# Block-sparse attention and a squared-ReLU feed-forward on one core: transposed scores, the mask in the contraction, row sums from a ones column, and two layers interleaved

## The chip, the core and the metric

The kernel runs on one core of one Trainium2 chip. The metric is the device time of one execution in microseconds (us). A profile of one execution gives, for each engine, every instruction's start, duration and what released it. PE is the matrix engine (TensorE), PEld its weight load, DVE is VectorE, ACT is ScalarE, POOL is GpSimd, SP is the engine whose queue issues most transfers here. The span of the profiled execution is 1.4 to 2.3 us shorter than its run time; stage lengths below are parts of the span.

## The reference

There are 4 batches, 8 heads, 768 tokens and 64 values per head. A query block of 32 tokens sees its neighbour blocks, the first and the last block, and three random blocks. The first and the last query block see everything. The result is reshaped to 3072 x 512 and goes through a two-layer feed-forward part with 2048 hidden units.

```python
scores = scale * np.matmul(q, k.transpose(0, 1, 3, 2))       # scale = 1/8
mask = np.abs(blk_i - blk_j) <= window                        # window = 1, blocks of 32
mask = mask | (blk_i == 0) | (blk_j == 0) | (blk_i == n_blocks - 1) | (blk_j == n_blocks - 1)
for qb in range(n_blocks):
    for kb in sampled_blocks[qb]:                             # 3 random blocks
        mask[qb * block:(qb + 1) * block, kb * block:(kb + 1) * block] = True
scores = np.where(mask, scores, -1000000000.0)
attn = softmax(scores)                                        # shortened
x = (attn @ v).transpose(0, 2, 1, 3).reshape(B * S, H * D)
h = x @ w_in
r = np.maximum(h, 0.0)
return (r * r) @ w_out
```

## The kernel before

It has three parts, one after the other. First a mask of 128 x 6 x 768 numbers is built. Then attention treats one tile of 128 queries and one head at a time: there are 192 such tiles. Queries lie on the partitions, so the probabilities have to be transposed before they can be multiplied with the values. Last comes the feed-forward part, for which the weights are loaded and cast in one go.

```python
# one tile of attention; 4 batches x 4 head pairs x 6 query tiles x 2 heads
ps_sc = psAsc.tile([P, S], F32, name="ps_sc", tag="ps_sc")          # one buffer
nc.tensor.matmul(ps_sc[:, :512], lhsQ, kT[hl][:, :512], start=True, stop=True)
nc.tensor.matmul(ps_sc[:, 512:], lhsQ, kT[hl][:, 512:], start=True, stop=True)
nc.scalar.activation(out=sc, in_=ps_sc, func=AF.Exp, scale=scale)
# ... cut
nc.vector.tensor_tensor_reduce(out=scb, in0=sc, in1=mask_add[:, qi, :], scale=1.0, scalar=0.0,
                               op0=AOP.mult, op1=AOP.add, accum_out=row_sum)
nc.vector.reciprocal(out=inv_sum, in_=row_sum)
for tch in range(TCH):                                              # 6 times
    nc.tensor.transpose(ps_tr, scb[:, tch * P:(tch + 1) * P], identb)
    nc.vector.tensor_copy(out=aT, in_=ps_tr)
    nc.tensor.matmul(ps_o, aT, vT[hl][:, tch, :], start=(tch == 0), stop=(tch == TCH - 1))
nc.vector.tensor_scalar_mul(out=pair_out[:, hl * D:(hl + 1) * D], in0=ps_o, scalar1=inv_sum)
# ... cut: output transpose and its copy into xT_sb

# feed-forward, after all of attention; 6 x 16 times
# ... cut: four matmuls into ps_gT
nc.scalar.activation(out=g, in_=ps_gT, func=AF.Relu)
nc.scalar.activation(out=gb, in_=g, func=AF.Square)
for ts in range(tw_per):
    nc.tensor.matmul(ps_y[ts], gb[:, ts * P:(ts + 1) * P], w_out_sb[:, nch, :],
                     start=(nch == 0), stop=(nch == NF - 1))
```

The softmax here doesn't subtract the row's maximum and nothing guards it: scores larger than these inputs give would overflow.

## Time and profile before

The median of three runs is 892.4 us; the span of the profiled one is 891.0 us.

| stage | span, us | what fills it |
|---|---|---|
| set-up | 0 to 63 | mask on DVE and PE |
| attention | 63 to 703 | 192 tiles at 3.33 us; PE and DVE both about 80% busy |
| feed-forward | 703 to 891 | PE 94% busy, DVE almost idle |

Over the span PE is busy for 730.3 us, DVE for 553.8, ACT for 270.2 and POOL for 4.5. Such a table must not be read as "PE has 18% to spare": in attention a tile is handed from PE to ACT to DVE to PE, and each waits for the other. The prediction below shows the lines for this.

### The profile page before, as it was taken

Reading aid. Unit: us, or ns where it says so; the run is one execution under the profiler, and the core shown is the slowest. Engines: PE = TensorE matmul, PEld = TensorE weight load, DVE = VectorE, ACT = ScalarE, POOL = GpSimd, SP = SyncE. Lnnn points to the kernel's source line nnn. Section 1 sums busy time; section 2 is a strip of 40 time slices with the busy share of each in tenths; the row PEclk is TensorE's granted clock in tenths of the full one; section 3 lists DMA queues with packets and bytes.
Section 4 is the critical chain, followed back from the end, with each engine's and each line's share of the span. In section 5 each row is a group of like instructions: output and inputs, shape, how many; then the busy total and the mean of one; then the engine's idle time right before and its main releaser. Section 6 shows DMA issues by size and latency. Waiting matters only on the chain.

```text
span 891.0 us, 12152 instructions
## 1 busy us (share of the span) xinstructions
PE 730.3 (82%) x3969; PEld 351.4 (39%) x3985; DVE 553.8 (62%) x2609; ACT 270.2 (30%) x385; POOL 4.5 (1%) x21
## 2 busy tenths in 40 slices
PE   3878878787888778787888778787878899999996
PEld 1223444444343444444343444444443333333332
DVE  6547877878787877878787878878786400110111
ACT  0013122131312222131313222121313266666664
POOL 2000000000000000000000000000000000000000
PEclk9999999999999999999999999999999999999999
DMA  9800101021120202021120202020100001110111
GB/s 273 263 0 1 28 1 36 1 54 30 25 54 1 54 1 54 1 54 27 28 47 8 54 0 54 1 54 22 24 1 0 1 1 48 47 48 1 48 47 48
DMA packets 81411, 34.33 MB, mean 39 GB/s; under 512 B 75716, under 2 KB 75716, under 8 KB 80836
## 3 DMA queue, kind: packets, MB, share of 16 engines
q1 hardware_dynamic: 81348, 33.56, 14.3%
q8 instruction: 31, 0.51, 0.2%
q14 instruction: 32, 0.26, 0.1%
HBM read 27.26 MB, written 6.29 MB: 38 GB/s over the span
## 4 chain that ended last, share of the span: by engine, by line
PE 50%; DVE 25%; ACT 19%; issue 4%; DMA 1%; another core or an unknown queue 0%; SPq 0%; DVEq 0%; ACTq 0%
DVE scb L175 12%; ACT sc L172 12%; PE ps_sc L169 10%; PE ps_y L223 10%; PE ps_o L186 8%; PE ps_tr L183 6%; PE ps_sc L170 5%; DVE aT L185 4%; ACT gb L221 4%; ACT g L219 3%; PE ps_gT L212 3%; PE ps_t L158 2%; DVE pair_out L188 2%; PE ps_t L161 2%; DVE kTb L162 2%
## 5 line engine op out<-in xcount | busy, mean ns | idle before, releaser
L172 ACT ACTIVATE sc<-ps_sc 128x768 f32<-128x768 f32 x192 | 155.8, 811 | 474.3 <-PE ps_sc L170 282.0
L185 DVE COPY aT<-ps_tr 128x128 bf16<-128x128 bf16 x1152 | 203.4, 221 | 104.8 <-PE ps_o L186 93.5
L183 PE MATMUL ps_tr<-identb,scb 128*128 128x128 bf16 x1152 | 224.6, 299 | 20.9 <-DVE xT_sb L192 14.2
L186 PE MATMUL ps_o<-vTb,aT 128*128 128x64 bf16 x1152 | 213.3, 245 | 17.5 <-DVE aT L185 8.9
L175 DVE CUSTOM_DVE_ANT_0 scb<-sc,mask_add 128x768 bf16<-128x768 f32 x192 | 181.4, 945 | 2.5 <-ACT sc L172 2.5
L186 PEld LDWEIGHTS <-aT 128*128 128x128 bf16 x1152 | 119.8, 112 | 160.2 <-DVE aT L185 112.8
L183 PEld LDWEIGHTS <-scb 128*128 128x128 bf16 x1152 | 140.1, 135 | 56.9 <-issue 29.8
L169 PE MATMUL ps_sc<-kTb,qTb 64*128 64x512 bf16 x192 | 113.1, 589 | 30.8 <-ACT sc L172 25.2
L227 DVE COPY y_sb<-ps_y 128x512 f32<-128x512 f32 x24 | 15.5, 687 | 170.6 <-PE ps_y L223 164.6
L223 PE MATMUL ps_y<-w_out_sb,gb 128*128 128x512 bf16 x377 | 100.0, 381 | 4.3 <-ACT gb L221 1.4
L212 PE MATMUL ps_gT<-xT_sb,w_in_sb 128*128 128x512 bf16 x375 | 100.7, 385 | 1.1 <-DVE xT_sb L192 0.3
L219 ACT ACTIVATE g<-ps_gT 128x512 f32<-128x512 f32 x96 | 56.6, 589 | 74.5 <-PE ps_gT L212 71.7
L170 PE MATMUL ps_sc<-kTb,qTb 64*128 64x256 bf16 x192 | 77.9, 406 | 0.0
L190 PE MATMUL ps_poT<-identb,pair_out 128*128 128x128 bf16 x96 | 27.7, 288 | 59.7 <-DVE pair_out L188 59.7
L188 DVE TENSOR_SCALAR pair_out<-ps_o,inv_sum 128x64 bf16<-128x64 f32 x192 | 54.2, 282 | 21.5 <-PE ps_o L186 17.7
L221 ACT ACTIVATE gb<-g 128x512 bf16<-128x512 f32 x96 | 60.5, 630 | 3.1
L223 PEld LDWEIGHTS <-gb 128*128 128x128 bf16 x384 | 30.2, 98 | 68.9 <-ACT gb L221 45.0
L158 PE MATMUL ps_t<-identb,qsb 128*64 128x128 bf16 x192 | 51.4, 286 | 6.3 <-DVE qsb L151 4.6
L212 PEld LDWEIGHTS <-w_in_sb 128*128 128x128 bf16 x384 | 38.0, 99 | 46.4 <-issue 2.7
L161 PE MATMUL ps_t<-identb,ksb 128*64 128x128 bf16 x192 | 51.4, 278 | 1.4 <-DVE ksb L152 1.4
L159 DVE COPY qTb<-ps_t 64x128 bf16<-64x128 bf16 x192 | 40.1, 209 | 5.6 <-PE ps_t L158 5.5
L190 PEld LDWEIGHTS <-pair_out 128*128 128x128 bf16 x96 | 10.0, 105 | 80.2 <-DVE pair_out L188 70.2
(53 smaller groups left out, 317.1 us busy)
## 6 DMA issues: line engine op xcount, KB each, us to landing
qs<-in_q_dram SPq DMA_DIRECT2D x32, 192.0 KB, 3.0
ks<-in_k_dram SPq DMA_DIRECT2D x32, 192.0 KB, 2.8
vs<-in_v_dram SPq DMA_DIRECT2D x32, 192.0 KB, 3.1
out_dram<-y_sb SPq DMA_DIRECT2D x24, 256.0 KB, 2.0
w_in_f<-in_moe_w_in_dram SPq DMA_DIRECT2D x1, 4096.0 KB, 13.7
w_out_f<-in_moe_w_out_dram SPq DMA_DIRECT2D x1, 4096.0 KB, 16.0
sb_i<-in_sampled_blocks_dram SPq DMA_DIRECT2D x1, 0.6 KB
```

Of the source, the lines that this page charges most:

```text
L169: nc.tensor.matmul(ps_sc[:, :512], lhsQ, kT[hl][:, :512], start=True, stop=True)
L170: nc.tensor.matmul(ps_sc[:, 512:], lhsQ, kT[hl][:, 512:], start=True, stop=True)
L172: nc.scalar.activation(out=sc, in_=ps_sc, func=AF.Exp, scale=scale)
L175: nc.vector.tensor_tensor_reduce(out=scb, in0=sc, in1=mask_add[:, qi, :], scale=1.0, scalar=0.0, op0=AOP.mult, op1=AOP.add, accum_out=row_sum)
L183: nc.tensor.transpose(ps_tr, scb[:, tch * P:(tch + 1) * P], identb)
L185: nc.vector.tensor_copy(out=aT, in_=ps_tr)
L186: nc.tensor.matmul(ps_o, aT, vT[hl][:, tch, :], start=(tch == 0), stop=(tch == TCH - 1))
L188: nc.vector.tensor_scalar_mul(out=pair_out[:, hl * D:(hl + 1) * D], in0=ps_o, scalar1=inv_sum)
L212: nc.tensor.matmul(ps_gT, w_in_sb[:, kc, nch * P:(nch + 1) * P], xT_sb[:, kc, tt4 * TW:(tt4 + 1) * TW], start=(kc == 0), stop=(kc == KM - 1),)
L219: nc.scalar.activation(out=g, in_=ps_gT, func=AF.Relu)
L221: nc.scalar.activation(out=gb, in_=g, func=AF.Square)
L223: nc.tensor.matmul(ps_y[ts], gb[:, ts * P:(ts + 1) * P], w_out_sb[:, nch, :], start=(nch == 0), stop=(nch == NF - 1))
```

## The change

The intent is to remove the transposes of probabilities and the mask multiplication, and to give every engine something to do at every time.

- Scores are computed transposed, with keys on the partitions. Their exponentials can then be used as they are in the value matmul.
- The contraction over 64 values leaves half of the 128 rows unused. 24 of them carry a one-hot code of the key block and the matching mask column of the query, so masked scores come out as about -8e9 and their exponential is 0.
- The value operand has a column of ones beside the 64 values, so the row sums come out of the same matmul. They then lie on one partition, and their reciprocals must be spread over 64. This is done with a transfer of the sums to a 16 x 96 tile (`st`), a reciprocal (`rc`), a transfer to DRAM (`rd`), and a broadcast back (`rt`).
- Work is cut into 16 units of two heads, nine steps each, 144 steps in all, one exponential of 128 x 1024 per step. The feed-forward part of a batch is laid between the steps of the next batch; the weights are loaded in 16 pieces during the first batch.

```diff
+    def spread(dst, src, lo):           # 24 rows of one-hot code or of mask, four of them for each of two operand sets
+        V.tensor_copy(out=dst[lo:lo + nb, :].rearrange("k (n p) -> k p n", p=P),
+                      in_=src[lo:lo + nb, :].unsqueeze(2).broadcast_to([nb, nb, block]))
... (cut)
-                    nc.tensor.matmul(ps_sc[:, :512], lhsQ, kT[hl][:, :512], start=True, stop=True)
-                    nc.tensor.matmul(ps_sc[:, 512:], lhsQ, kT[hl][:, 512:], start=True, stop=True)
-                    nc.scalar.activation(out=sc, in_=ps_sc, func=AF.Exp, scale=scale)
-                    nc.vector.tensor_tensor_reduce(
-                        out=scb, in0=sc, in1=mask_add[:, qi, :], scale=1.0, scalar=0.0,
-                        op0=AOP.mult, op1=AOP.add, accum_out=row_sum)
-                    for tch in range(TCH):
-                        nc.tensor.transpose(ps_tr, scb[:, tch * P:(tch + 1) * P], identb)
-                        nc.vector.tensor_copy(out=aT, in_=ps_tr)
-                        nc.tensor.matmul(ps_o, aT, vT[hl][:, tch, :], start=(tch == 0), stop=(tch == TCH - 1))
... (cut)
+    def scores(s):                      # twice per step: two heads, 128 keys x 256 queries
+            nc.tensor.matmul(ps[:, c, 0, :], KA[i][0:64 + nb, ksl], QA[i][0:64 + nb, qsl], start=True, stop=True)
+            nc.tensor.matmul(ps[:, c, 1, :], KB[i][:, ksl], QB[i][:, qsl], start=True, stop=True)
+        nc.scalar.activation(out=pT, in_=ps, func=AF.Exp, scale=scale)
+    def values(s):                      # two steps later; VA and VB hold the ones column
+            nc.tensor.matmul(po[:, 0, :], VA[i][:, n, :], pT[:, c, 0, :], start=first, stop=last, ...)
+            nc.tensor.matmul(po[:, 1, :], VB[i][:, n, :], pT[:, c, 1, :], start=False, stop=last, ...)
+            V.tensor_copy(out=etile[u][:, :, qi * QW:(qi + 1) * QW], in_=po)     # every third step
... (cut)
-            nc.scalar.activation(out=g, in_=ps_gT, func=AF.Relu)
-            nc.scalar.activation(out=gb, in_=g, func=AF.Square)
+        V.tensor_scalar(out=r, in0=ph, scalar1=0.0, scalar2=None, op0=AOP.max)
+        G.tensor_mul(out=g, in0=r, in1=r)                                        # POOL
... (cut)
+        e = s0 + SPU + 2                # s0: first of the unit's nine steps
+        at(e, lambda u=u: sums_out(u))
+        at(e + 2, lambda u=u: recip(u))
+        at(e + 2, lambda u=u: spread_recip(u))
+        at(e + 6, lambda u=u: normalize(u))
+    for i in range(2 * NWP):            # 16 weight pieces, two staging buffers, same SP queue
+        at(9 + 2 * i // 2, lambda i=i: w_load(i))
+        at(12 + 2 * i // 2, lambda i=i: w_cast(i))
```

## The prediction

> **What bounds the kernel now.** I read the slices first, to see stages:
>
> ```profile
> PE   3878878787888778787888778787878899999996
> DVE  6547877878787877878787878878786400110111
> ACT  0013122131312222131313222121313266666664
> PEclk9999999999999999999999999999999999999999
> ```
>
> Two regimes: attention, where PE and DVE are both near 8 and neither is full, and from slice 32 a feed-forward part with PE at 9 and DVE idle. The boundaries from the timeline are 63 us (first exp), about 703 us (first feed-forward matmuls) and 891 us, so I asked for busy time by stretch:
>
> ```profile
> core 0: us, PE busy (x) PEld busy (x) DVE busy (x) ACT busy (x) POOL busy (x), PEclk, DMA share, GB/s
> 0.00:63.00 63.00, 39.89 (x75) 12.29 (x76) 34.57 (x125) 1.16 (x1) 4.47 (x21) 1.00 0.66 189
> 63.00:383.00 320.00, 257.08 (x1577) 136.07 (x1577) 252.24 (x1232) 78.37 (x98) 0.00 (x0) 1.00 0.11 26
> 383.00:703.00 320.00, 256.08 (x1569) 135.59 (x1569) 251.53 (x1229) 77.53 (x96) 0.00 (x0) 1.00 0.11 24
> 703.00:891.00 188.00, 177.20 (x751) 67.41 (x764) 15.47 (x24) 113.11 (x192) 0.00 (x0) 0.99 0.09 34
> ```
>
> Set-up is 63 us, attention 640 us (3.33 us for each of its 192 tiles of 128 queries by one head), feed-forward 188 us. In attention DVE has 504 of 640 us (79%). The chain that ended last and the groups say why nothing is full there:
>
> ```profile
> DVE scb L175 12%; ACT sc L172 12%; PE ps_sc L169 10%; PE ps_y L223 10%; PE ps_o L186 8%; PE ps_tr L183 6%; PE ps_sc L170 5%; DVE aT L185 4%; ACT gb L221 4%; ACT g L219 3%; PE ps_gT L212 3%; PE ps_t L158 2%; DVE pair_out L188 2%; PE ps_t L161 2%; DVE kTb L162 2%
> ...
> L172 ACT ACTIVATE sc<-ps_sc 128x768 f32<-128x768 f32 x192 | 155.8, 811 | 474.3 <-PE ps_sc L170 282.0
> L185 DVE COPY aT<-ps_tr 128x128 bf16<-128x128 bf16 x1152 | 203.4, 221 | 104.8 <-PE ps_o L186 93.5
> ...
> L175 DVE CUSTOM_DVE_ANT_0 scb<-sc,mask_add 128x768 bf16<-128x768 f32 x192 | 181.4, 945 | 2.5 <-ACT sc L172 2.5
> ...
> L227 DVE COPY y_sb<-ps_y 128x512 f32<-128x512 f32 x24 | 15.5, 687 | 170.6 <-PE ps_y L223 164.6
> ...
> L219 ACT ACTIVATE g<-ps_gT 128x512 f32<-128x512 f32 x96 | 56.6, 589 | 74.5 <-PE ps_gT L212 71.7
> ```
>
> The chain alternates DVE, ACT and PE (25%, 19%, 50% of the span): each tile goes scores, exp, mask multiply, six transposes, six copies, six value matmuls, and there is one score buffer in PSUM. The exp group waited 474 us in all. DVE's masked multiply and transpose copies alone are 181.4 + 203.4 us. Attention is bound by this hand-to-hand chain with DVE as its heaviest link; feed-forward by PE with short waits for ACT.
>
> The last view is the pace of matmuls, because PE busy time counts latencies. In attention a 512-column matmul is followed by the next one 0.40 us later:
>
> ```profile
> 303.85 0.60 PE L169 MATMUL ps_sc<-kTb,qTb 64*128 64x512 bf16 x1
> 304.25 0.42 PE L170 MATMUL ps_sc<-kTb,qTb 64*128 64x256 bf16 x1
> ```
>
> At the start of feed-forward, and then 9 us later:
>
> ```profile
> 702.72 3.51 PE L212 MATMUL ps_gT<-xT_sb,w_in_sb 128*128 128x512 bf16 x8 [0.22 <-issue]
> ...
> 711.76 1.67 PE L212 MATMUL ps_gT<-xT_sb,w_in_sb 128*128 128x512 bf16 x7
> ```
>
> Eight matmuls in 3.51 us, 0.43 us apart, then seven in 1.67 us: (1.67 - 0.38)/6 = 0.215 us apart. PE ran at half pace through attention and the first 4 us of feed-forward, although the clock row shows 9 throughout.
>
> **What the Trainium skill says.** "TensorE: Matmul & The Clock Gate", Back-to-back issue gap: N/2.4 + 2.5 ns warm (216 for N=512), N/1.2 cold (427). The trace agrees with both, 215 and 430. The same page, Part 4: PE-mode transpose, says that transposes don't count as PE activity for the clock; that fits an attention stage full of transposes staying cold. "GPSIMD Engine Reference", 3.1, measures a two-input f32 tensor_tensor of 2048 elements at 4497 ns, 2.2 ns per element; this trace has none on POOL. "SBUF — State Buffer", Who interferes with whom: GpSimd shares a port pair with DVE and locks out DVE's two-port copies and two-input operations, one blocking the other for an instruction; this trace can't show it.
>
> **The change, part by part.** *Removed:* 1152 probability transposes and their 1152 copies, the 192 mask multiplies, the per-tile reciprocals, scalings and output transposes. On DVE that is 203.4 + 181.4 + 29.4 + 54.2 + 21.2 + 15.9 = 505 us of 554. The mask rides in unused contraction rows, the row sums in a ones column, so PE pays nothing for either: a score or value matmul costs its columns. Also gone: most of the mask set-up and the serial feed-forward.
>
> *PE after,* at the warm pace (0.215 us per 512 columns; N=256 and N=384 scaled, 0.108 and 0.161): 144 steps of eight 256-column matmuls = 1152 x 0.108 = 124 us; 192 input transposes at 0.13 (their spacing around 300 us in the trace) = 25; hidden layer 512 x 0.161 = 82; output layer 384 x 0.215 = 83. Sum 314 us.
>
> *ACT after:* 768 columns take 811 ns and 512 take 589, so 0.867 ns each; a 1024-column exp is 811 + 256 x 0.867 = 1033 ns. 144 x 1.033 = 149, plus 24 output copies of about 0.59 = 14: 163 us.
>
> *DVE after:* f32 from PSUM is 687 ns for 512 and, for mask_add, 952 for 768, so a 384-column relu is 555 ns; 128 of them 71 us. A unit (two heads, nine steps) has two casts at 0.55 (interpolated between 350 ns for 384 columns and 4405 for 8192), two value casts at 0.35, four 64x768 evictions at 0.55 to 0.88 (the copy slope at double or single rate), three 0.687 evictions, two 768-column two-input multiplies at 0.945 and a small reciprocal: 8.2 to 9.6 us, some 0.95 us a step. Weight casts: 16 x 0.68 = 11. In all about 235 us. *POOL after:* 128 squares of 384, estimated from the skill page at 384 x 2.2 = 0.84 us, 108 us.
>
> No engine's sum exceeds PE's 314, but the order matters. The instruction order has four phases:
>
> 1. *Set-up.* DVE makes the one-hot and mask rows: some 16 tiny operations, then eight strided 24x768 spreads at about 0.95 (the single-rate copy) = 7.6 us, then casts and evictions, after a first load landing near 4 us. First exp near **19 us** (63 before).
> 2. *Attention alone,* 46 steps (36 of batch 0, then a lag of 10). ACT's 1.03, PE's 0.86 + 0.17 and DVE's 0.95 are nearly equal, and DVE sits in order behind waits for small transfers (sums out, reciprocals to DRAM and back, each about 2 to 3 us to land as the transfers of before do), and one output accumulator makes PE wait for DVE. I take 1.2 us a step for 30 of them, 36 us. For 16 steps a 512 KB weight piece is loaded and cast per step with two staging buffers: 4096 KB landed in 13.7 us, so a piece needs 1.7 us plus about 1.6 of latency, and with two in flight a pair takes about 4.1 us including its cast. 16 x 2.05 = 33 us. With 3 us at the cold clock: **72 us**. The weight loads are the wait that I expect to be new.
> 3. *Interleaved,* 108 steps, bound by PE. Step with batch 0's feed-forward: 0.86 + 0.17 + (32 x 0.64 + 12 x 0.86)/36 = 1.89 us, times 36 = 68. With batches 1 and 2: the bracket is (20.5 + 20.6)/36 = 1.14, step 2.17, 78 each; the last ten steps lack scores, nearly all values and transposes, so minus 9. Sum 215, plus 5% for DVE-POOL locks, the shared h buffers and the single output-layer bank: **226 us**.
> 4. *Tail,* batch 3's feed-forward alone: 32 x 0.64 + 36 x 0.86 = 51.5, plus waits for the last square, copy and transfer (2.03 us at the end of before): **57 us**.
>
> 19 + 72 + 226 + 57 = 374 us.
>
> **The rivals.** *(a) POOL becomes the bound of the feed-forward.* Against it: 0.84 us against 1.9 to 2.2 us for PE per step. For it: no trace here has this operation, and it can be locked out by DVE. At 1.6 us a square the tail is unchanged to +10 and the interleaved part loses little: 385 to 395. *(b) DVE is the bound with its in-order waits,* because single-rate evictions, locks and transfer waits add up to over 2 us a step. For it: 1.44 us of work a step in phase 3 already. If it adds 0.3 us a step to 108 steps, 405 to 410. *(c) The clock stays cold in attention alone,* since PE waits half of each step in the weight-load part. At 0.215 a matmul of 256, a step is 1.72 + 0.2 us; the 30 other steps gain 0.7 us each: 395. Against it: PE has matmuls, not transposes, for over 70% of such a step. *(d) The weight loads are hidden,* transfers overlapping better than two at a time: attention alone shrinks to 55 us, total 355. *(e) Nothing gained by interleaving,* which would leave attention at 144 x 1.2 and feed-forward at 170: about 365 to 370, so the prediction hardly depends on it.
>
> **Range and chances.** The PE sum plus set-up and an idle front of 25 us is a floor near 345; (b) and (c) together come to about 425. Most surprises lengthen it, so the range leans up: 374 us, 350 to 412. For less than 2% gain the new kernel would have to exceed 874 us, more than twice the PE sum: faster 0.99.
>
> **What would show it.** Right: first exp near 19 us; exps every 1.2 us at first, about 2 us apart during the weight casts with DVE waiting for staged weights; then PE at 9 with ACT around half and matmuls of 256 columns 0.11 us apart; a tail of 50 to 57 us with ACT nearly idle. Wrong: POOL squares well over 1.2 us with relu waiting for POOL; score matmuls 0.21 us apart; DVE at 9 in the interleaved part, PE's output or h matmuls waiting for it; or exps 1.03 us apart straight through the weight loads.

## The result, and the profile after

The changed kernel took 392.39 us (median of four runs, 392.2 to 396.8). The kernel before took 892.51 us in the same rounds (892.33 to 893.23). The ratio is 0.441, with a 95% interval from 0.439 to 0.443. Here and below a ratio is the mean time of one kernel's fast runs over that of the other's of the same rounds, so it is not quite the ratio of the medians that are quoted. Executions over 1.5% slower than the fastest of the same kernel are left out of the means.

The first view is the page's table of 40 slices (9.76 us each) of the changed kernel, with the busy share in tenths:

```profile
PE   0048627347889889999999999999999997999995
DVE  7975625337677868677777667767665465444410
POOL 5000000000004643233324343333433433666530
PEclk9999865688989999999999999999999999999999
```

From slice 16 on PE is at 9, but for a 7 in slice 34 and the last slice. The front is different: two slices without PE, then a hole, 2, 7, 3 and 4 in slices 6 to 9, where the granted clock also falls to 5 or 6. I cut the span at the events of the prediction (first exponential 26.9, first hidden-layer matmul 116.6, end of the last attention step 331.9), and cut the second stage twice more. The columns are those of the prediction's view of stretches: stretch and length, busy time of PE, PEld, DVE, ACT and POOL with the number of instructions, the granted clock, the share of the transfer engines, and GB/s.

```profile
0.00:26.90 26.90, 2.68 (x18) 1.90 (x19) 23.87 (x34) 1.28 (x1) 5.75 (x21) 1.00 0.39 127
26.90:47.00 20.10, 15.46 (x133) 12.62 (x132) 10.69 (x21) 14.73 (x15) 0.00 (x0) 0.99 0.49 158
47.00:92.00 45.00, 22.82 (x128) 16.58 (x126) 21.17 (x34) 13.57 (x14) 0.00 (x0) 0.66 0.64 204
92.00:116.60 24.60, 19.09 (x164) 15.59 (x163) 15.79 (x28) 16.98 (x18) 0.00 (x0) 0.93 0.48 153
116.60:331.90 215.30, 208.21 (x1514) 144.54 (x1533) 148.36 (x246) 108.26 (x114) 80.33 (x94) 1.00 0.27 86
331.90:390.40 58.50, 52.90 (x267) 26.45 (x271) 18.27 (x33) 5.27 (x9) 27.70 (x34) 1.00 0.11 41
```

| stage | predicted, us | measured, us | difference |
|---|---|---|---|
| set-up | 19 | 26.9 | +7.9 |
| attention alone | 72 | 89.7 | +17.7 |
| interleaved | 226 | 215.3 | -10.7 |
| tail | 57 | 58.5 | +1.5 |
| sum | 374 | 390.4 | +16.4 |

In the interleaved part PE is busy for 208.2 of 215.3 us. In the middle of attention alone ACT made 14 exponentials in 45 us, 3.2 us each, while PE was busy for 51% of the time, DVE for 47% and ACT for 30%. The page's groups give the cost of one instruction (busy time, mean ns of one, then idle time before them and what ended it):

```profile
L246 ACT ACTIVATE pT<-ps 128x1024 bf16<-128x1024 f32 x144 | 145.8, 1023 | 161.8 <-PE ps L244 161.7
L315 POOL TENSOR_TENSOR g<-r 128x384 bf16<-128x384 f32 x128 | 108.0, 851 | 261.3 <-DVE r L313 261.3
```

The exponential (1023 ns; predicted 1033) and the square on POOL (851; predicted 840) are as worked out. In the groups by shape, one instruction is not:

```profile
L148 DVE CAST KA<-oh 24x768 bf16<-24x768 f32 x2 | 3.7, 1868 | 0.0
```

This is a spread of mask rows in set-up. It takes 1868 ns, where the prediction had about 950.

Now the stage in which most was lost. The waits of attention alone, longest sums first (engine and tile, what it waited for, then us in total, times, and the longest; a wait that began before the stretch is counted whole):

```profile
ACT pT L246 <- PE ps L244: 69.2, 32, 24.9
...
PE po L260 <- DVE et L267: 32.1, 13, 7.1
DVE rc L284 <- DMA st<-et: 13.1, 4, 5.8
DVE w_in_sb L218 <- DMA wst<-in_moe_w_in_dram: 9.2, 3, 6.8
DVE w_out_sb L221 <- DMA wst<-in_moe_w_out_dram: 6.3, 3, 4.4
```

ACT's longest wait, 24.9 us, is the one before the first exponential and belongs to set-up; 44.3 us are left for this stage, half of it. ACT waits for PE, PE for DVE to empty the one output accumulator (`et` from `po`), and DVE for two transfers: the row sums and the weight pieces. The timeline shows one such chain (start, duration, engine, line, operation, in brackets the idle time before it and what ended it; SPq is the queue of SP):

```profile
49.49 0.54 SPq L292 DMA_DIRECT2D rt<-rd  x1
50.76 9.91 SPq L208 DMA_DIRECT2D wst<-in_moe_w_in_dram  x4
...
56.33 0.69 DVE L218 CAST w_in_sb<-wst 128x1024 bf16<-128x1024 f32 x1 [6.84 <-DMA wst<-in_moe_w_in_dram]
...
57.80 0.37 PE L260 MATMUL po<-pT,VA 128*128 128x256 bf16 x1 [7.14 <-DVE et L267]
...
59.76 1.02 ACT L246 ACTIVATE pT<-ps 128x1024 bf16<-128x1024 f32 x1 [7.99 <-PE ps L244]
```

SP issues in order. The reciprocals go to DRAM at 45.50, and `rt` can only be issued when they have landed, at 49.49. The weight piece that DVE needs next stands behind it and is issued at 50.76, although a staging buffer was free when the cast at 46.26 ended, at 46.95. It then took 5.6 us to land. DVE stands for 6.84 us at the cast, in order, and the eviction that PE wants is the instruction behind the cast. So 6.84 us of DVE become 7.14 of PE and 7.99 of ACT.

After such a pause PE also restarts slowly. Where the matmul after this pause starts at 57.80, the next ones follow 0.21 us apart; at 93 us, after a pause of only 0.64 us, they follow 0.11 apart. In this stage there are 333 distances between neighbouring 256-column matmuls, of which 99 were at the slow pace (over 0.17 us): at the very start, then in runs of about 3 us after pauses (78.2 to 80.9, 88.4 to 91.1, and others), and in one of 12.7 us (58.0 to 70.7) with another pause of 2.53 us inside. The Trainium skill, "TensorE: Matmul & The Clock Gate", What's actually happening, describes a clock that falls to half after an idle window of about 3.4 us and rises after a busy one; the pauses of 5.69 to 7.14 us before these three runs agree. Two others, at 47.4 and 111.6, began 1.5 us after pauses of only 2.66 and 1.94 us.

The trace's own record of the granted clock explains these two. It changes only on a fixed grid of 3.41 us (half from 46.8 to 50.2, 53.6 to 70.7, 74.1 to 80.9, 87.7 to 91.1 and 111.6 to 115.0), and the slow runs lie in these stretches. The changes go with PE's idle time within one window of the grid. In the traces of this kernel and of all experiments, no window at full clock with less than 1.88 us of idle PE was followed by half clock, and none with more than 1.96 by full clock; from half clock it rose after windows with at most 0.53 us of idle PE, and not after those with 0.67 or more. So a pause of 1.94 us inside one window (108.2 to 111.6) halved the clock, while one of 1.91 us that is split over two (96.2 to 98.1) did not. One caution: before the first entry of this record, at 29.7 us here and at 706.0 in the kernel before, the views show full clock although the matmuls are at the slow pace.

### The profile page after: what moved, and what is told of

It reads as the page before. It is cut to its first block, busy times and chain, and to the rows that moved or that the text cites. A ratio compares the mean times of both kernels' runs of the same rounds, so it can differ in the third digit from the quotient of the medians.

```text
span 390.4 us, 5784 instructions
## 1 busy us (share of the span) xinstructions
PE 321.2 (82%) x2215; PEld 217.7 (56%) x2240; DVE 238.2 (61%) x392; ACT 160.1 (41%) x169; POOL 113.8 (29%) x149
## 4 chain that ended last, share of the span: by engine, by line
PE 62%; DVE 16%; DMA 14%; issue 3%; SPq 2%; ACT 1%; POOL 1%; DVEq 0%; ACTq 0%
PE py L325 19%; PE ph L310 17%; PE po L260 6%; PE po L262 6%; PE ps L244 6%; PE ps L242 6%; DMA st<-et 4%; DVE r L313 2%; DMA wst<-in_moe_w_in_dram 2%; DVE et L267 2%; PE pt L191 2%; DMA wst<-in_moe_w_out_dram 2%; DMA rd<-rc 2%; DMA sb_i<-in_sampled_blocks_dram 1%; DMA qs<-in_q_dram 1%
## 5 line engine op out<-in xcount | busy, mean ns | idle before, releaser
L246 ACT ACTIVATE pT<-ps 128x1024 bf16<-128x1024 f32 x144 | 145.8, 1023 | 161.8 <-PE ps L244 161.7
L315 POOL TENSOR_TENSOR g<-r 128x384 bf16<-128x384 f32 x128 | 108.0, 851 | 261.3 <-DVE r L313 261.3
L313 DVE TENSOR_SCALAR r<-ph 128x384 f32<-128x384 f32 x128 | 70.8, 556 | 71.1 <-PE ph L310 52.6
L310 PE MATMUL ph<-xT,w_in_sb 128*128 128x384 bf16 x512 | 100.9, 325 | 4.1 <-DVE r L313 3.4
L260 PE MATMUL po<-pT,VA 128*128 128x256 bf16 x288 | 75.5, 287 | 33.9 <-DVE et L267 33.9
L325 PE MATMUL py<-w_out_sb,g 128*128 128x512 bf16 x359 | 92.9, 379 | 3.1 <-ACT ys L329 1.4
L242 PE MATMUL ps<-QA,KA 88*128 88x256 bf16 x288 | 76.5, 288 | 1.4 <-DVE KA L193 1.2
L244 PE MATMUL ps<-QB,KB 128*128 128x256 bf16 x288 | 76.0, 286 | 0.3 <-DVE KB L194 0.3
L262 PE MATMUL po<-pT,VB 128*128 128x256 bf16 x288 | 75.7, 287 | 0.0
L325 PEld LDWEIGHTS <-g 128*128 128x128 bf16 x384 | 36.9, 97 | 35.0 <-issue 3.4
L242 PEld LDWEIGHTS <-KA 88*128 88x128 bf16 x288 | 29.7, 103 | 6.7 <-DVE KA L193 1.4
```

The source lines that it names most:

```text
L242: nc.tensor.matmul(ps[:, c, 0, :], KA[i][0:64 + nb, ksl], QA[i][0:64 + nb, qsl], start=True, stop=True)
L244: nc.tensor.matmul(ps[:, c, 1, :], KB[i][:, ksl], QB[i][:, qsl], start=True, stop=True)
L246: nc.scalar.activation(out=pT, in_=ps, func=AF.Exp, scale=scale)
L260: nc.tensor.matmul(po[:, 0, :], VA[i][:, n, :], pT[:, c, 0, :], start=first, stop=last, skip_group_check=True)
L262: nc.tensor.matmul(po[:, 1, :], VB[i][:, n, :], pT[:, c, 1, :], start=False, stop=last, skip_group_check=True)
L310: nc.tensor.matmul(ph, w_in_sb[:, kc, f * P:(f + 1) * P], xT[b][:, kc, t * TW:(t + 1) * TW], start=(kc == 0), stop=(kc == KM - 1))
```

## The experiments

All edits are against the changed kernel. The recorded texts give theories letters; A and its variants hold the weight pieces responsible for attention alone, L is about POOL keeping DVE from its port, Q about the order of the SP queue, and R about reading the row sums later. Below, "attention alone" is the time from the first exponential to the first hidden-layer matmul. All twelve runs were compared with the kernel before on the same chip; the changed kernel was not run again beside them, so differences to it are taken across rounds, in which the kernel before took 892.5 to 893.0 us. Each result was correct unless its text says that it is wrong.

### 1. No weight pieces at all (wrong)

```diff
-    for i in range(2 * NWP):
-        at(9 + 2 * i // 2, lambda i=i: w_load(i))
-        at(12 + 2 * i // 2, lambda i=i: w_cast(i))
+    G.memset(w_in_sb, 0.03)             # POOL
+    G.memset(w_out_sb, 0.03)
```

> No weight piece is loaded or cast; both weight matrices are filled with a constant on POOL, so the result is wrong on purpose. In the changed kernel the attention-alone part takes 89.7 us for 46 steps, of which the 14 steps around the weight pieces take 45 us. Theory A (weight pieces with in-order waits on SP and DVE cause the excess): every step returns to about 1.2 to 1.4 us, attention alone is 55 to 63 us, the whole 356 to 366 us. Rival B (the cold clock causes it, and the weights are a bystander): matmuls of 256 columns stay 0.21 us apart, steps near 1.8 us, attention alone above 80 us, the whole above 380. Rival C (the reciprocal's round trip through DRAM causes it): attention alone above 75 us, the whole above 375.

Measured: 378.25 us, ratio to the kernel before 0.424; first exponential at 39.9 us, attention alone 65.6. So attention alone became 24.1 us shorter, but the set-up 13.0 us longer. The experiment was confounded by my own edit. In its timeline:

```profile
6.63 6.92 POOL L380 MEMSET w_in_sb<- 128x8192 bf16 x1
7.10 6.49 DVE L144 TENSOR_SCALAR t<-t 128x24 f32<-128x24 f32 x1
```

A DVE operation on 24 columns, which takes about 0.2 us elsewhere, lasted for 6.49 us and ended when the POOL fill ended. A spread beside the second fill took 8.56. This agrees with the Trainium skill, "SBUF — State Buffer", Who interferes with whom: an instruction of one of the two engines can block the other for its whole length. The prediction could only quote that; here it is seen. Experiment 5 repeats this without POOL.

### 2. Six staging buffers for the weights

```diff
-        st = ld.tile([P, 1024], F32, name="wst", tag="wst")
+        st = ld.tile([P, 1024], F32, name="wst", tag="wst", bufs=6)
```

> Six staging buffers for weight pieces in place of two, nothing else. Theory A1 (the pieces are late because their issue waits for a free buffer): DVE's waits for staged weights, 15.5 us in the changed kernel, go to nearly nothing and the whole falls to 374 to 380 us. Rival A2 (the transfers themselves, about 200 GB/s in that stretch, or the order of small transfers behind large ones on the one SP queue set the pace): the wait moves from the weights to the row sums on their way out, and the whole stays within 386 to 394 us.

Measured: 382.28 us (0.429); attention alone 81.9, 7.8 us shorter. That is half-way between what the theories expect. Two buffers are part of the cause, and not all of it: PE still waited 24.5 us for DVE's eviction (32.1 before), and DVE 11.3 us for weight pieces (15.5 before), 6.4 of them at once, and 9.0 us for row sums (13.1 before).

### 3. Weight casts on POOL, transfers as they are

```diff
-            V.tensor_copy(out=w_in_sb[:, kc, hf * 1024:(hf + 1) * 1024], in_=st)
+            G.tensor_copy(out=w_in_sb[:, kc, hf * 1024:(hf + 1) * 1024], in_=st)
... (the same for w_out_sb)
```

> The sixteen weight casts move from DVE to POOL, which is idle there; loads, queue and buffers stay. Theory A3 (what hurts is that DVE, in order, stands before a cast and so evicts no accumulator): DVE loses 15.5 us of waits and 11 us of work, attention alone falls from 89.7 to about 70 us, the whole to 370 to 375 us. Rival A2 (the transfers set the pace through the SP queue): the row sums still land late, DVE waits for them in the reciprocal, 382 to 390 us.

Measured: 390.81 us (0.437); attention alone 86.5, only 3.2 us shorter. DVE no longer stands at a weight cast, but this is in its list of waits, the largest:

```profile
DVE rc L284 <- DMA st<-et: 28.1, 4, 16.5
```

The wait for row sums rose from 13.1 to 28.1 us, the longest from 5.8 to 16.5. In the longest one the row sums were ready at 54.7 us, stood in the SP queue behind weight pieces that wait for a free staging buffer until 65.3, and needed another 5.2 us to land after their last issue at 66.1. So DVE's place at the cast was not the whole cause; taking it away alone moved the wait to the next thing that comes through the same queue.

### 4. The second set of mask rows copied from the first

```diff
+        else:
+            V.tensor_copy(out=KA[i][64:64 + nb, :], in_=KA[0][64:64 + nb, :])
... (the same for KB, QA and QB; the spreads only for i == 0)
```

> The one-hot and mask rows of the second set of operand buffers are copied from the first set (four contiguous copies of 24x768, estimated 0.3 us each) in place of four more strided spreads of 1.87 us. If the set-up is DVE's chain and nothing hides it, the first exp moves from 26.9 to about 20.6 us and the whole falls by 6.3 us to 386 us. If the first loads or POOL's filling set the first exp, less than 2 us is gained.

Measured: 386.38 us (0.432; the fast runs spread from 383.5 to 386.8, the slow one took 389.9), first exponential at 21.1 us, 5.8 earlier. Four spreads of 1.87 us became four contiguous copies of 0.35, which is 4 x 1.52 = 6.1 us. The same bytes on the same 24 partitions take a fifth of the time. The copy is contiguous, but it also reads bf16 where the spread reads repeated f32 numbers; how much the stride alone costs was not separated. (A contiguous cast of 768 f32 columns takes 0.55 us.) Its profiled run was slow (388.1 us span), so its trace is used only for these durations on DVE and for the first exponential, which comes at 20.6 in the fast runs 9, 10 and 12 with the same edit.

### 5. No weight pieces, filled by ACT (wrong)

```diff
-    for i in range(2 * NWP):            # loads and casts, as in experiment 1
+    nc.scalar.copy(out=w_in_sb.rearrange("p k f -> p (k f)"), in_=cst.broadcast_to([P, KM * d_ff]))
+    nc.scalar.copy(out=w_out_sb.rearrange("p k f -> p (k f)"), in_=cst.broadcast_to([P, NF * d_model]))
```

> The same question as the first run without weights, without its fault: there POOL filled the weights while DVE was in its set-up, and the first exp slipped from 26.9 to 39.9 us. Here ACT, idle until the first exp, fills them with a constant (wrong result on purpose). Theory A (weight pieces cost attention alone some 24 us): first exp again at 27 us, attention alone 64 to 67 us as in that run, the whole 365 to 370 us. Theory L (POOL's long fills locked DVE out): DVE's small set-up operations are back at under 0.7 us each although 14 us of filling goes on beside them. Rival: the first exp is late again, or the whole stays above 376.

Measured: 365.68 us (0.409); first exponential at 26.2, as in the changed kernel, and so the late start of experiment 1 came from the POOL fills. Attention alone is one line of its stretches:

```profile
26.20:93.30 67.10, 52.91 (x421) 42.65 (x420) 36.94 (x65) 44.77 (x46) 0.00 (x0) 0.92 0.35 115
```

67.1 us for 46 steps, 1.46 each. The weight pieces cost 89.7 - 67.1 = 22.6 us. The rest is over the prediction too: 46 steps at 1.2 and 3 us for the clock are 58.

### 6. Weights on another queue: POOL issues and casts, six buffers

```diff
-            nc.sync.dma_start(out=st, in_=wiv[:, kc, hf * 1024:(hf + 1) * 1024])
+            nc.gpsimd.dma_start(out=st, in_=wiv[:, kc, hf * 1024:(hf + 1) * 1024])
... (the same for w_out; casts as in 3, buffers as in 2)
```

> Weight pieces are issued on POOL's own queue, cast by POOL, with six staging buffers: nothing of them is left in SP's or DVE's order. Theory Q (the excess of the weight stretch is the one SP queue: small transfers of the row sums stand behind weight pieces, which stand behind casts, and DVE stands in the reciprocal; three-fold remedies must be taken together): DVE's wait for row sums falls to about 10.5 us as without weights, attention alone to 65 to 70 us, the whole to 366 to 372 us. Rival A2 (transfer bandwidth): the same 8.4 MB still has to pass in the same time, so 380 us or more. A third way: POOL's casts lock DVE out and give 10 us back.

Measured: 376.48 us (0.421), above the 366 to 372 expected. Attention alone is 61.7 us, 28.0 shorter, and DVE waits 10.5 us for row sums, as without weights. This fits the theory of the queue's order, but queue, buffers and casts were changed together. POOL, no longer behind SP's or DVE's order, also issued its first piece at 6.6 us (24.2 in the changed kernel), so that ten of the sixteen casts ran in set-up. A fairer count is from the start: the first hidden-layer matmul came at 99.8 us, 16.8 earlier than in the changed kernel (116.6) and 6.5 later than with no weights at all (93.3). But the set-up grew to 38.1 us. The timeline has the reason:

```profile
17.50 4.39 DVE L148 CAST KB<-oh 24x768 bf16<-24x768 f32 x1
17.60 1.05 POOL L218 CAST w_in_sb<-wst 128x1024 bf16<-128x1024 f32 x1
```

POOL now reached its casts during set-up, and the spread beside them took 4.39 us in place of 1.87. So a part of the gain was given back by the same block between POOL and DVE, the third way of the recorded text.

### 7. Not interleaved: feed-forward after all of attention

```diff
-            queue += list(mlp((s - LAG) // (HP * SPU) - 1))
+            late += list(mlp((s - LAG) // (HP * SPU) - 1))
... (cut: all of late runs at the end; xT has four buffers)
```

> No interleaving: the feed-forward of all batches runs after the last attention step, everything else as in the changed kernel. Theory I (interleaving is worth its keep, because attention alone takes about 1.4 us a step of which PE works 1.0): 98 steps x 1.4 = 137 us plus 128 x 0.65 + 96 x 0.86 = 166 us take the place of 215 + 58, so about 418 us (410 to 426). The prediction's rival (e) (nothing gained by interleaving, PE is nearly full in either order): 385 to 396 us.

Measured: 453.42 us (0.507; one of its four runs was slow), 61.0 us more than the changed kernel and 35 more than expected. Attention took 236.7 us in all. Its last 98 steps, from the 47th exponential at 119.4 us to the last at 261.4, long after the last weight piece, took 1.46 us each. The stretch that begins just before:

```profile
116.00:262.90 146.90, 115.33 (x932) 93.75 (x931) 87.56 (x148) 99.07 (x101) 0.00 (x0) 0.90 0.32 103
```

No engine is over 80% busy there. DVE waited 41.1 us for row sums in the whole stage and PE 65.4 for DVE's eviction. From 150 us on the trace shows the same pattern every 13.7 us, once per unit (1.52 us a step): a pause of about 1.9 us before a value matmul, some 11 distances at the slow pace, then 54 at the fast one. Attention alone does not run at the 1.2 us a step that I had assumed. Beside feed-forward matmuls the same pauses are filled.

Most of the miss lies elsewhere: the feed-forward part took 190.2 us where 166 were expected. At its start DVE, in order, stood behind the last unit's round trip, so PE waited 11.5 us for the first relu (264.4 to 275.8 us), and PE's clock was at half until 281. That belongs to the seam in this edit's order, and not to running the parts apart as such.

### 8. As 6, with reciprocals two steps later and the multiplication one

```diff
-        at(e + 2, lambda u=u: recip(u))
-        at(e + 2, lambda u=u: spread_recip(u))
-        at(e + 6, lambda u=u: normalize(u))
+        at(e + 4, lambda u=u: recip(u))
+        at(e + 4, lambda u=u: spread_recip(u))
+        at(e + 7, lambda u=u: normalize(u))
```

> As the run with weights on POOL, and the reciprocal and its spreading come four steps after the row sums leave in place of two, the multiplication seven steps after in place of six. Theory R (what is left above 1.1 us a step is DVE standing in order before row sums that need about 3.5 us to land): DVE's wait in the reciprocal falls from 10 us to under 3, attention alone loses 6 to 9 us against that run. Rival (the steps are set by PE's cold clock or by ACT): the wait goes and the time stays within 2 us of that run.

Measured: 391.12 us (0.438), 14.6 us worse than experiment 6; attention alone 70.6. The reciprocal no longer waits, as wanted, but the multiplication by `rt` has only three steps left for the way to DRAM and back, and waits 2.4 to 2.7 us each time. At the start of the feed-forward part PE waits another 5.1 us for the normalized tile. The theory missed: the wait moved on by one station, and there it stands in front of the casts of the next queries and keys and of an eviction. The waits themselves are no larger (10.5 us for row sums in 6, 8.8 for `rt` here), so they don't account for the loss by their sums.

### 9. Set-up and the first batch together

```diff
+    NPRE = 6                            # casts held back until the first operands are there
+    for i in range(NPRE):
+        w_load(i)
+    G.tensor_copy(out=mark[D:P, :], in_=KB[0][D:P, 0:1])
... (weights as in 6, mask rows as in 4)
-            otile[u, qi] = ps_o.tile([P, 2, QW], F32, name="po", tag="po")
+            if u < HP and (u * NQ + qi) % 2:         # first batch: second accumulator in the idle output bank
+                otile[u, qi] = ps_y.tile([P, d_model], F32, name="py", tag="y")...
```

> Three remedies together: the second set of mask rows copied instead of spread; weights on POOL's queue and cast by POOL, the first six pieces issued at once, but the casts held back until the first keys stand in their operand buffer, so that they can't lock DVE out of the set-up; in batch 0 the accumulator of values alternates between its own bank and the output layer's, which is idle then. If the set-up of the run with weights on POOL (38.1 us) was long through the lock, the first exp is now at 21 us. If PE's 13 us of waits for the accumulator in attention alone came from its single buffer, attention alone falls from 61.7 to 52 to 57 us. Sum with the unchanged 274 us after it: 347 to 353 us. If the accumulator waits only hide DVE standing at the reciprocal, attention alone stays near 62 and the whole at 357.

Measured: 365.10 us (0.409). The set-up is as expected, first exponential at 20.6, because POOL's casts now wait until DVE has finished the first operands. Attention alone was missed: 67.3 us. DVE waited 15.8 us for row sums, the longest wait 8.1; the mean granted clock was 0.87. Counted from the start, the first hidden-layer matmul came at 87.9 us, 11.9 earlier than in 6.

### 10. As 9, with a longer round trip for the first three units

```diff
+        d1, d2 = (4, 9) if u < HP - 1 else (2, 6)
+        at(e + d1, lambda u=u: recip(u))
+        at(e + d1, lambda u=u: spread_recip(u))
+        at(e + d2, lambda u=u: normalize(u))
```

> As the run before it, and for the first three units the reciprocal comes four steps and the multiplication nine steps after the row sums leave (two and six in the changed kernel), so that both legs of the round trip have time: the earlier try with four and seven only moved DVE's wait to the multiplication, 2.5 us each. Theory R2 (DVE's in-order waits for this round trip are what is left above ACT's 1.03 us a step): DVE's waits for both legs fall from about 10 to under 4 us, attention alone to 47 to 52 us, the whole to 342 to 348 us. Rival (ACT and the cold start already bound it): within 2 us of the run before it.

Measured: 359.31 us (0.403); attention alone 63.2. Both ends of the round trip were given time here, unlike in 8, and it gained 5.8 us over 9, less than expected. From 28.5 to 37.1 us nine exponentials started 0.95 us apart on average, most of them just before the end of the last. Then:

```profile
40.41 6.63 DVE L173 CAST qc<-qs 128x768 bf16<-128x768 f32 x1
40.68 5.95 POOL L225 CAST w_out_sb<-wst 128x1024 bf16<-128x1024 f32 x6
```

POOL made six casts one after the other, and a DVE cast of 0.55 us took 6.63 and ended after the last of them.

### 11. As 10, each POOL cast held back until an exponential has run

```diff
+        G.tensor_copy(out=mark, in_=ptile[1 + 2 * i][:, 0, 0, 0:1])
+        w_cast(i)                       # one every two steps
```

> As the last run, but each weight cast on POOL waits for an exp, one in two steps, so that POOL never runs casts back to back. In the last run a DVE cast that takes 0.55 us took 6.63 us beside six POOL casts in a row, and ACT then sat idle for 4 us. Theory L (the shared port: POOL's consecutive instructions keep DVE's two-port copies out): no DVE cast of queries or keys over 2 us, attention alone 63.2 to 57 to 60 us, the whole 353 to 357 us. Rival (DVE was held by something else, such as the late load): the cast stays long and the whole at 359 us.

Measured: 362.17 us (0.405); attention alone 65.8. The block is gone: the longest such DVE cast is 1.55 us (1.83 in run 12). But DVE then waited 5.59 us, until 49.05, for the first unit's `rt`, which had been issued at 42.47, and nothing was gained.

### 12. As 11, fourth unit included, feed-forward three steps later

```diff
-        d1, d2 = (4, 9) if u < HP - 1 else (2, 6)
+        d1, d2 = (4, 9) if u < HP else (2, 6)
-    LAG = 10
+    LAG = 13
```

> As the run before it; also the fourth unit of batch 0 gets the long round trip (four and nine steps), and the feed-forward starts three steps later (lag 13 in place of 10) so that it has its input. In the last run DVE stood 2.5 us at this unit's reciprocal and ACT 7 us before the next exp. Theory R2: both waits go, the 49 steps before the first feed-forward matmul take about 53 us, and as the three steps are only moved, the whole is 349 to 353 us. Rival (the start of the feed-forward three steps later costs what is gained): within 2 us of the run before it.

Measured: 358.70 us (357.3 to 358.9; 0.401), 8.6% under the changed kernel and the lowest median of all, though not clear of run 10 (358.7 to 361.4); the set-up ends at 20.6 and attention alone takes 63.1 us for 49 steps, 1.29 each. The expected time was missed again, but in this direction there was a gain of 3.5 us over 11. DVE's wait for the first `rt` is still there, 5.8 us.

### The runs side by side

The time is the median of a run's executions. The stages are those of the one that was profiled, which can be up to 3.8 us off the median, so small differences between stages are not safe to read.

| run | time, us | set-up, us | attention alone, us | rest of the span, us |
|---|---|---|---|---|
| changed kernel | 392.4 | 26.9 | 89.7 | 273.8 |
| 1 no weights, POOL fills | 378.3 | 39.9 | 65.6 | 274.8 |
| 2 six buffers | 382.3 | 26.2 | 81.9 | 271.2 |
| 3 casts on POOL | 390.8 | 26.4 | 86.5 | 274.3 |
| 4 rows copied (stages of a slow run) | 386.4 | 21.1 | 91.3 | 275.7 |
| 5 no weights, ACT fills | 365.7 | 26.2 | 67.1 | 274.2 |
| 6 own queue | 376.5 | 38.1 | 61.7 | 274.7 |
| 8 own queue, later | 391.1 | 37.9 | 70.6 | 280.7 |
| 9 front | 365.1 | 20.6 | 67.3 | 276.0 |
| 10 front, round trip | 359.3 | 20.6 | 63.2 | 273.3 |
| 11 paced casts | 362.2 | 21.2 | 65.8 | 276.4 |
| 12 paced, later start | 358.7 | 20.6 | 63.1 | 273.1 |

The last column hardly moves, except in run 8 with its late normalized tiles. Nearly everything that these edits gained or lost lies in front of the first hidden-layer matmul. (Experiment 7 has no such division; in 12 three more steps lie in attention alone.)

## Why the prediction was right or wrong

The direction and the range were right: 392.4 us lies in 350 to 412. The point of 374 was 18.4 us too low: 16.4 us of the span, and 2.0 us of run time outside it, which the sum did not have. Term by term:

**Removed work: right.** DVE's total fell from 553.8 to 238.2 us (235 worked out), ACT's from 270.2 to 160.1 (163), and the mask and the row sums cost PE nothing but their columns. The relu took 556 ns (555), POOL's squares 108.0 us in all (108).

**Set-up, 19 us: a wrong size.** The step that failed is "eight strided 24x768 spreads at about 0.95 (the single-rate copy) = 7.6 us". A spread took 1.87 us. Eight times 0.92 is 7.3 of the 7.9 us. The rate of a contiguous copy was carried over to a copy that writes every 256 bytes. Experiment 4 confirms that these copies set the first exponential: with four of them replaced it came 5.8 us earlier.

**Attention alone, 72 us: the mechanism named, its sizes too small, in two halves.** The weight loads were "the wait that I expect to be new", and they were. The failed step is "16 x 2.05 = 33 us"; in the stretch from 47 to 92 us an exponential came every 3.2 us. The prediction took transfers and buffers as a pipeline of their own. In fact they share one queue, in order, with the row sums and reciprocals of the attention, and they share DVE, in order, with the eviction that PE waits for. Over the 1.2 us of a plain step the prediction had 16 x 0.85 = 14 us for the weights; experiment 5 against the changed kernel gives 22.6. What queue and buffers do together is shown by 6 against 3: casts on POOL in both, own queue, an earlier first issue and six buffers in 6, and the first hidden-layer matmul at 99.8 against 112.9 us, although the set-up of 6 is 11.7 us longer. Six buffers alone (2) brought it to 108.1. Own queue and buffers were not separated further, so how much the queue alone is worth stays open.

The other half is "1.2 us a step". Without any weights a step took 1.46 us (5), and long after the weights, without feed-forward beside it, also 1.46 (7). The three engines' sums per step, 0.9 to 1.03 us, were right, but a nearly balanced step has no room for a round trip that stops DVE once a unit. In experiment 7, 98 steps at 1.46 took 26 us more than they would have at 1.2.

**Interleaved, 226 us: the 5% was not needed.** The PE sum without stalls was 215, and 215.3 was measured. Rival (a), POOL as the bound, is out: a square took 0.851 us and POOL was busy for 80 of 215 us. Rival (b), DVE as the bound, is out: 148.4 of 215.3 us. PE's waits for DVE's eviction are 33.9 us in the whole kernel, and 32.1 of them lie in attention alone; without interleaving they were 65.4. Beside feed-forward work PE has other matmuls to do meanwhile. That the total came within 18 us is partly luck: the 10.7 us that were not needed here offset a part of the 25.6 lost in front.

**Tail, 57 us: right,** 58.5, with ACT busy for 5.3.

**Rival (c), the cold clock: half right.** It does not "stay cold", it falls after each long pause and comes back after a window with hardly any pause: most runs lasted 2.6 to 3.3 us, one 12.7. The argument against it was off too: PE was to have matmuls for "over 70%" of such a step, and was busy for 51% of the stretch. The 99 slow distances cost 99 x (0.213 - 0.110) = 10.2 us of PE time, an upper limit of what it cost the stage. The best version has 38 of them, 3.9 us. What of it was on the path was not measured by itself. A hint is 6 against 5: DVE waits 10.5 us for row sums in both and PE 13.0 and 13.9 us for evictions, but the granted clock was 0.97 against 0.92, and the stage 5.4 us shorter. It follows from the pauses; removing these removes most of it.

**Rival (d), weights hidden: not in this kernel.** In experiment 6 attention alone, at 61.7 us, was shorter than without any weights (67.1), but ten of the sixteen casts had moved into a longer set-up.

**Rival (e), nothing gained by interleaving: wrong, and with a wrong number.** "144 x 1.2 and feed-forward at 170" gave 365 to 370, a sum that leaves out the prediction's own 14 us for weights and 3 for the clock (with these and set-up it is 378); the run without interleaving took 453.4. Interleaving is worth 61 us in this comparison. Some 14 of them, an estimate from 11.5 us of pause and 5 us at half clock, are the seam of experiment 7. The rest fits PE's work filling the pauses of an attention that alone takes 1.46 us a step, at a granted clock of 0.90 in place of 1.00. The prediction said that it "hardly depends" on this rival, but only because it took 1.2 us for a step of attention alone.

**Still open.** The best version needs 1.29 us a step in attention alone, against 1.02 for the exponential (0.95 where they follow each other directly in run 10). In experiments 8 to 12 DVE's wait moved between the row sums, the reciprocals' return and the block by POOL, and all five took longer than I had expected. One cause is in the traces: weight pieces slow the small transfers on another queue too. In run 10, with the weights on POOL's queue, `rt` is issued as soon as `rd` has landed. For the first two units this is:

```profile
38.80 0.36 SPq L293 DMA_DIRECT2D rd<-rc  x1
42.37 0.53 SPq L299 DMA_DIRECT2D rt<-rd  x1
...
53.17 0.34 SPq L293 DMA_DIRECT2D rd<-rc  x1
54.57 0.51 SPq L299 DMA_DIRECT2D rt<-rd  x1
```

That is 3.57 us while 261 GB/s were moving, and 1.40 once the weights were in (4 GB/s). Runs 9, 11 and 12 have 3.2 to 3.6 for the first unit and 1.4 for the next three, and experiment 5, without weights, 1.4 for all. How much of the remaining 0.27 us a step this explains was not tested.

## What to carry to other kernels

A small transfer on the way of the data should not share an in-order queue, nor an in-order engine, with bulk loads that wait for free buffers: look in the profile for who stands *behind* a waiting instruction, not only at what waits. When one wait of a chain is removed, expect the next station of the same round trip to take its place, and give time to all of its ends at once. Another queue takes a small transfer out of the bulk loads' order, but not out of their traffic (3.57 against 1.40 us here). Interleaving two parts is worth most where one of them has pauses that its engine sums do not show, so measure the part alone before taking its sums for its pace.

## What the Trainium skill lacked or had wrong

- "SBUF — State Buffer", Who interferes with whom: the block of DVE by POOL for a whole instruction agrees (a 0.2 us operation took 6.49 us beside a fill of 6.92). Missing is that back-to-back POOL instructions don't let DVE in between: a cast of 0.55 us took 6.63 beside six casts of 0.99 us each.
- "SBUF — State Buffer", Door 1: The DMA port swizzle, notes a penalty for each access that crosses to a new 16-byte line, without a figure for DVE. Here a DVE cast of 24 x 768 that writes 2 bytes every 256 took 1868 ns, 2.4 ns per element, against 0.55 us for a contiguous cast of 768. That this penalty is the reason was not tested.
- "DMA: Bandwidth & Descriptors", Issuing engines are not separate DMA queues, says that issuing from several engines only saves the time to initiate a transfer. It lacks that an in-order queue whose head waits for a buffer or for another transfer holds up everything behind it: the longest wait for 3 KB of row sums was 16.5 us in experiment 3, and with the weights on POOL's queue and six buffers (experiment 6, both at once) the first hidden-layer matmul came 13.1 us earlier.
- "TensorE: Matmul & The Clock Gate", Back-to-back issue gap, gives about 131 ns as a sustained spacing for 512 columns beside the formula with 216. The traces show 215 for 512 columns and 108 to 110 for 256, as in the formula, and nothing near 131.
- "TensorE: Matmul & The Clock Gate", What's actually happening: half pace after an idle window of about 3.4 us agrees for pauses of 5.69 to 7.14 us, but here half pace also followed pauses of 1.94 and 2.66 us. It lacks how much idle time in a window suffices: here every window of 3.41 us at full clock with more than 1.96 us of idle PE was followed by half clock, and none with less than 1.88. The page's section A second HAM failure mode describes a clock that swings with frequent short idles, without a figure for how short they may be.
- "DMA: Bandwidth & Descriptors", Anatomy of one DMA, gives a fixed cost of about 2.0 us for a transfer issued by GpSimd. Here, issued by SP, from the issue of the 6 KB of reciprocals to DRAM to that of the broadcast, which waits for them, 1.4 us went by with nothing else in flight (at 96.37 and 108.44 us) and 4.0 and 3.1 us with weight pieces in flight (at 45.50 and 77.66).
